# Two row blocks of a seven-product output step finished in their PSUM bank, and weight sums made four steps later

## The chip, the core and the metric

One core of a Trainium2 chip runs the whole program in one launch. The metric is device time in microseconds, the median of several runs; a profiled execution of the same program gives the traces. Engines are PE (matrix unit; PEld are its weight loads), DVE (vector), ACT (scalar), POOL (GpSimd) and SP (here only a queue that issues DMAs). Each works off its instructions in the order in which the program wrote them.

## What is computed

Attention with keys and values projected along the sequence, and behind it a gated feed-forward block:

```python
k_proj = einsum('ks,bhsd->bhkd', E, k)          # 1024 positions -> 64
v_proj = einsum('ks,bhsd->bhkd', F, v)
attn   = softmax(q @ k_proj^T / sqrt(64))       # 8 batches, 8 heads, 1024 x 64
x      = (attn @ v_proj), heads side by side    # 8192 rows x 512
g      = x @ w_gate                             # 512 -> 1536
out    = (g * sigmoid(g) * (x @ w_val)) @ w_out # 1536 -> 512, float32
```

## The kernel before

Rows are worked in 16 chunks c of 512 (`NC`), two to a batch. A chunk has 12 steps f (`NFT`), one for each 128 columns of the hidden layer, and the main loop counts them as t = 12c + f. In each step `f_g` makes four matmuls into the gate bank (`gps`, L462) and ACT the tanh `th` (L474); `f_v` makes four into the value bank (`vps`, L462), and DVE makes `s` (L481) from `th` and `gps` and `hT` (L486) from `s` and `vps`. There are two buffers for `gps` and two for `vps`, so the gate matmuls of step t need that `s` of step t-2 is done.

The order of everything else is written out by hand. `slots` holds, for two places in each step, the attention work of later batches: loads by POOL's DMA queue (`load_k`, `load_v`, `load_q`), key and value projections (`kvp`, L162), transposes by SP's DMA queue (`u_TD` makes `qTd`, `u_AD` makes `AT`), scores (`sc`, L353, `ee`), softmax sums on DVE (`zz` L368, `rr` L370), the scaling on POOL (`AAd`, L383) and the product with the values (`pv`, L410). `late` holds what runs after `f_v` of a step: the output product.

Chunk 0 takes its output product directly (`f_y`, L498, in t = 16 to 23). Chunks 1 to 15 take it as a 2 x 2 block product in seven block products instead of eight: the hidden layer in two halves and the output columns in two halves, the rows in two halves too. The sums of blocks that this needs are made ahead: of `w_out` by `w_sum` (`ws`, DVE, L526, five instructions for the whole run), of `hT` by `h_sum` (`hs`, L547; numbers 5 and 2 on POOL step by step, 1, 6 and 7 on DVE in the first steps of the next chunk). `f_m` takes one product per step while the next chunk is worked, n = 0 to 13: for each half p of the 128-row blocks the products 3, 4, 5, 2, 1, 6, 7, each six matmuls of 128x256 (`yps`, L564). With M1 to M7 for the products, the four output blocks are

```
C12 = M3 + M5          C21 = M4 + M2
C11 = M1 + M7 + M3 + M4 - C12      C22 = M1 + M6 + M3 + M4 - C21
```

In the kernel before, four banks' worth of products go through two PSUM banks, "y" and "z": X = [M3, M4] in y, Y = [M5, M2] in z, W = M1 in y, Z = [M7, M6] in z. `m_X` copies X to `xs` on ACT (L581) and adds its two halves to `tt` on POOL (L584); `m_Y` makes C12 and C21 on DVE (L590); `m_W` adds M1 to `tt` on DVE (L597); `m_Z` subtracts C12 and C21 from Z on DVE (`dd`, L603), and POOL adds `tt` to both (L604). SP then sends the four blocks (L610). Each of these stands right behind the product that completes its bank. The products stand in steps 0, 1, 2, 3, 4, 5, 5 for the first half and 6 to 11, 11 for the second, so that 6 and 7 share a step.

The last chunk has no chunk behind it: `f_m_last` makes its 14 products back to back, with the last additions of the first half on DVE, and of the second half in two pieces (L652, L658) whose rows ACT's DMA queue sends (L659).

The five `w_sum` stand in steps 2 to 6 of chunk 1. `wo` is `w_out` in SBUF, loaded by two DMAs on POOL's queue in the start-up.

Of the kernel before, what the change touches and what calls it, by code (L numbers as in the profile page):

```python
# [10 lines left out]
ALU = mybir.AluOpType  # L11
AX = mybir.AxisListType
BF16 = mybir.dt.bfloat16
FP32 = mybir.dt.float32
# [8 lines left out]
P = 128  # L23
# [5 lines left out]
CW = 512  # L29
# [3 lines left out]
HC = DM // 2  # L33
# [5 lines left out]
def kernel(  # L39
# [19 lines left out]
    nc = tc.nc  # L59
    scale = 1.0 / float(D) ** 0.5  # L60

    const = ctx.enter_context(tc.tile_pool(name="const", bufs=1))
# [6 lines left out]
    fw = ctx.enter_context(tc.tile_pool(name="fw", bufs=3))  # L69
    y_pool = ctx.enter_context(tc.tile_pool(name="ysb", bufs=2))  # L70
    d_pool = ctx.enter_context(tc.tile_pool(name="dsb", bufs=2))
# [4 lines left out]
    ps_a = ctx.enter_context(tc.tile_pool(name="psa", bufs=2, space=bass.MemoryType.PSUM))  # L76

    ident_bf = const.tile([P, P], BF16, name="ident_bf")
    ident_fp = const.tile([P, P], FP32, name="ident_fp")
    BD = [const.tile([P, H, P], BF16, name=f"BD{i}") for i in range(2)]  # L80
    BDV = [const.tile([P, NPAIR, P], BF16, name=f"BDV{i}") for i in range(2)]
    ks = [const.tile([P, H, D], BF16, name=f"ks{i}") for i in range(2)]
# [11 lines left out]
    def load_k(b, h0=0, h1=H):  # L94
        if b:
            kb[b] = kv_pool.tile([P, H, NJ, D], BF16, name="kb", tag="kb")
        nc.gpsimd.dma_start(
            out=kb[b][:, h0:h1].rearrange("p h j d -> p h (j d)"),
            in_=k[b, h0:h1].rearrange("h (p j) d -> p h (j d)", j=NJ),
        )  # L100
# [41 lines left out]
    def bank(where, shape, dt, name):  # L142
        if where == "a" and ring["wide"]:
            where = "aaz"[ring["n"] % 3]
            ring["n"] += 1
        pool, tag = banks[where]
        return pool.tile(shape, dt, name=name, tag=tag)
# [217 lines left out]
    def u_R(b, u):  # L365
        e = ee[b, u]
        z = aw.tile([P, 4, 2], FP32, name="zz", tag="zz", bufs=3)
        nc.vector.reduce_sum(out=z[:], in_=e[:], axis=AX.X)  # L368
        r = aw.tile([P, 4, 2], FP32, name="rr", tag="rr", bufs=4)
# [79 lines left out]
    half = {}  # L449
# [60 lines left out]
    def rows_of(c):  # L510
        b, ch = divmod(c, CH)
        return out[b * S : (b + 1) * S, :].rearrange("(p c j) d -> p c j d", c=CH, j=4)[:, ch]
# [38 lines left out]
            op=op,  # L551
        )

    def m_mm(c, p, m, ps):

        for f in range(HF):
            if m == 3:
                lhsT = hT[c][:, f, p * P : (p + 1) * P]
            elif m == 4:
                lhsT = hT[c][:, HF + f, HT + p * P : HT + (p + 1) * P]  # L560
            else:
                lhsT = hs[c, m][:, f, p * P : (p + 1) * P]
            rhs = {2: wo[:, f, 0:HC], 5: wo[:, HF + f, HC:DM]}.get(m)
            nc.tensor.matmul(  # L564
                out=ps,
                lhsT=lhsT,
                rhs=ws[m][:, f, :] if rhs is None else rhs,
                start=(f == 0),
                stop=(f == HF - 1),
            )  # L570

    ym = {}

    def m_bank(c, p, which, at):
        t = ym[c, p, which] = bank(at, [P, 2, HC], FP32, "yps")
        return t

    def m_X(c, p):

        xs = d_pool.tile([P, 2, HC], FP32, name="xs", tag="d")  # L580
        nc.scalar.copy(out=xs[:], in_=ym.pop((c, p, "X"))[:])  # L581
        ym[c, p, "xs"] = xs
        t = d_pool.tile([P, HC], FP32, name="tt", tag="t", bufs=2)
        nc.gpsimd.tensor_tensor(out=t[:], in0=xs[:, 0], in1=xs[:, 1], op=ALU.add)  # L584
        ym[c, p, "T"] = t

    def m_Y(c, p):

        ysb = ym[c, p, "y"] = y_pool.tile([P, 4, HC], FP32, name="ysb", tag="ysb")
        nc.vector.tensor_tensor(  # L590
            out=ysb[:, 1:3], in0=ym.pop((c, p, "xs"))[:], in1=ym.pop((c, p, "Y"))[:], op=ALU.add
        )

    def m_W(c, p):

        t = ym[c, p, "T"]
        nc.vector.tensor_tensor(out=t[:], in0=t[:], in1=ym.pop((c, p, "W"))[:, 0], op=ALU.add)  # L597

    def m_Z(c, p, eng=nc.gpsimd):

        d = d_pool.tile([P, 2, HC], FP32, name="dd", tag="d")
        ysb = ym[c, p, "y"]
        nc.vector.tensor_tensor(out=d[:], in0=ym.pop((c, p, "Z"))[:], in1=ysb[:, 1:3], op=ALU.subtract)  # L603
        eng.tensor_tensor(  # L604
            out=ysb[:, 0::3],
            in0=d[:],
            in1=ym.pop((c, p, "T"))[:].unsqueeze(1).to_broadcast([P, 2, HC]),
            op=ALU.add,
        )
        nc.sync.dma_start(  # L610
            out=rows_of(c)[:, p::2, :], in_=ym.pop((c, p, "y"))[:].rearrange("p (j x) d -> p j (x d)", j=2)
        )

    def f_m(c, n):

        p, n = divmod(n, 7)
        m = (3, 4, 5, 2, 1, 6, 7)[n]
        which, at, half = (
            ("X", "y", 0), ("X", "y", 1), ("Y", "z", 0), ("Y", "z", 1), ("W", "y", 0), ("Z", "z", 1), ("Z", "z", 0),
        )[n]  # L620
        if n in (0, 2, 4, 5):
            m_bank(c, p, which, at)
        m_mm(c, p, m, ym[c, p, which][:, half])
        if n in (1, 3, 4, 6):
            {1: m_X, 3: m_Y, 4: m_W, 6: m_Z}[n](c, p)

    def f_m_last(c):

        X = [m_bank(c, p, "X", "yg"[p]) for p in range(2)]
        Z = [m_bank(c, p, "Z", "a") for p in range(2)]  # L630
        Y = [m_bank(c, p, "Y", "vz"[p]) for p in range(2)]
        m_mm(c, 0, 3, X[0][:, 0])
        m_mm(c, 0, 6, Z[0][:, 1])
        m_mm(c, 1, 6, Z[1][:, 1])
        m_mm(c, 1, 3, X[1][:, 0])
        for p in range(2):
            m_mm(c, p, 4, X[p][:, 1])
            m_X(c, p)
        for p in range(2):
            m_mm(c, p, 5, Y[p][:, 0])  # L640
            m_mm(c, p, 2, Y[p][:, 1])
            m_Y(c, p)
        W = [m_bank(c, p, "W", "gv"[p]) for p in range(2)]
        m_mm(c, 0, 1, W[0][:, 0])
        m_W(c, 0)
        m_mm(c, 0, 7, Z[0][:, 0])
        m_mm(c, 1, 1, W[1][:, 0])
        m_Z(c, 0, nc.vector)
        m_W(c, 1)
        ysb, t = ym[c, 1, "y"], ym[c, 1, "T"]  # L650
        d = d_pool.tile([P, 2, HC], FP32, name="dd", tag="d")
        nc.vector.tensor_tensor(  # L652
            out=d[:], in0=t[:].unsqueeze(1).to_broadcast([P, 2, HC]), in1=ysb[:, 1:3], op=ALU.subtract
        )
        for x in (1, 0):
            if x == 0:
                m_mm(c, 1, 7, Z[1][:, 0])
            nc.vector.tensor_tensor(out=ysb[:, 3 * x], in0=d[:, x], in1=Z[1][:, x], op=ALU.add)  # L658
            nc.scalar.dma_start(  # L659
                out=rows_of(c)[:, 1 + 2 * x, :], in_=ysb[:, 2 * x : 2 * x + 2].rearrange("p x d -> p (x d)")  # L660
            )


    slots = defaultdict(list)
# [37 lines left out]
    with tc.manual_schedule():  # L702
# [3 lines left out]
        for i in range(2):  # L706
            nc.scalar.dma_start(
                out=kraw[i][:],
                in_=k[0, 2 * i : 2 * i + 2].rearrange("h (p j) d -> p h (j d)", j=NJ),
# [5 lines left out]
        nc.sync.dma_start(out=ef[0][:], in_=E)  # L715
        load_q(0, 0, (0, 2))
        load_k(0, 4, 8)
        zeros = const.tile([P, CW], BF16, name="zeros")
        nc.vector.memset(zeros[:], 0.0)
        make_identity(nc, ident_fp[:])  # L720
        make_identity(nc, ident_bf[:])
# [34 lines left out]
        for h in range(4):  # L756
            for n in range(2):
                eng = act if (h, n) == (3, 1) else dve
# [76 lines left out]
        for b in range(2, B):  # L835
            s0 = 48 * (b - 1) - (20 if b == 3 else 24)
            at = (43, 43, 44, 45) if b == 2 else (s0, s0 + 2, s0 + 4, s0 + 6)
# [9 lines left out]
        late = defaultdict(list)  # L847
        for n in range(NFT):
            late[NFT + 4 + (2 * n + 1) // 3].append((f_y, 0, n))
        for m, f in ((3, 2), (4, 3), (6, 4), (7, 5), (1, 6)):  # L850
            late[NFT + f].append((w_sum, m))
        for c in range(1, NC):
            for f in range(HF):
                for m in (5, 2):
                    late[c * NFT + HF + f].append((h_sum, c, m, f, f + 1))
            if c == NC - 1:
                late[c * NFT + HF].append((h_sum, c, 6, 0, HF, nc.vector))
                for f in (0, 2, 4):
                    for m in (1, 7):
                        late[c * NFT + HF + f + 1].append((h_sum, c, m, f, f + 2, nc.vector))  # L860
            else:
                for i, m in enumerate((1, 6, 7)):
                    late[(c + 1) * NFT + 1 + i].append((h_sum, c, m, 0, HF, nc.vector))
                for n, f in enumerate((0, 1, 2, 3, 4, 5, 5, 6, 7, 8, 9, 10, 11, 11)):
                    late[(c + 1) * NFT + f].append((f_m, c, n))

        for t in range(NIT):
            c, f = divmod(t, NFT)
# [5 lines left out]
            for fn, *a in late.pop(t, ()):  # L874
                fn(*a)
            run_slot(2 * t + 1)
        f_m_last(NC - 1)
        assert not slots and not late

# [28 lines left out]
```

## Time and profile before

| | |
|---|---|
| median of 3 runs | 556.84 us (556.82 to 557.48) |
| the profiled execution's own time | 556.68 us |
| its span, first to last instruction | 554.92 us |
| mean granted PE clock | 0.994 of full speed |
| busy: PE, DVE, ACT, POOL | 542.1, 428.5, 216.2, 291.6 us |
| PE instructions | 3500 matmuls, 3500 weight loads |
| HBM read, written | 60.29 MB, 16.78 MB |

A busy time is the sum of the durations of an engine's instructions without overlaps. A matmul's duration includes its way through the array (128x512 shows 0.378 us in the mean), while the next one starts after 0.216 us; so PE's pace is read from starts. In a timeline line the two numbers at the front are the start and the duration, and a bracket tells how long the engine was idle before and what ended that. A wait line gives the engine and line that waited, what released it, and then total, number and longest.

### The profile page before, as it was taken

The page shows a single profiled execution, that of the slowest core. Times are in us where ns is not written, and L with a number is a line of the kernel's source. Part 1 is how long each engine was busy: PE and PEld are TensorE (multiplying, and loading weights), DVE is VectorE, ACT ScalarE, POOL GpSimd, SP SyncE. Part 2 cuts the span into 40 slices and gives each one's busy share as a digit, 9 for nine tenths or more (in the row PEclk, how much of TensorE's full clock was granted, in tenths as well). Part 3 has the DMA queues.
Part 4 walks back from the last instruction along what each step waited for, and adds up shares of the span by engine and source line. Part 5 has one row for each costly group of instructions (what it writes and reads, how often), then busy time and mean ns, then how long its engine had stood idle before and what let it go on. Part 6 is the DMA issues. An engine that isn't in the chain of part 4 may idle for free.

```text
span 554.9 us, 9311 instructions
## 1 busy us (share of the span) xinstructions
PE 542.1 (98%) x3500; PEld 318.3 (57%) x3500; DVE 428.5 (77%) x726; ACT 216.2 (39%) x386; POOL 291.6 (53%) x364
## 2 busy tenths in 40 slices
PE   8999899999999999999999999999999999999995
PEld 4654355556556655556556655566655665555664
DVE  3785886779678875988669896788859887776894
ACT  3564343253435333453334424254244433333220
POOL 6851194376627835187443856258451763516162
PEclk9999899999999999999999999999999999999998
DMA  9999949918961599036970399313990212110012
GB/s 203 192 198 190 172 97 194 189 39 143 194 120 41 100 187 206 1 76 121 205 130 1 77 176 200 81 40 85 180 192 38 73 50 69 40 39 22 17 39 113
DMA packets 111613, 62.86 MB, mean 113 GB/s; under 512 B 65872, under 2 KB 102736, under 8 KB 111568
## 3 DMA queue, kind: packets, MB, share of 16 engines
q0 software_dynamic: 43952, 29.49, 37.2%
q1 hardware_dynamic: 66784, 31.20, 25.4%
q10 hardware_dynamic: 832, 1.57, 0.9%
q8 instruction: 27, 0.44, 0.3%
q14 instruction: 18, 0.15, 0.1%
HBM read 60.29 MB, written 16.78 MB: 139 GB/s over the span
## 4 chain that ended last, share of the span: by engine, by line
PE 87%; DMA 8%; POOL 2%; DVE 1%; issue 1%; ACT 0%; POOLq 0%; DVEq 0%
PE vps L462 27%; PE gps L462 27%; PE yps L564 24%; DMA wo<-in_moe_w_out_dram 4%; PE sc L353 2%; PE pv L410 2%; PE kvp L162 2%; PE yps L498 2%; DMA qb<-in_q_dram 2%; DMA Fraw<-in_F_dram 1%; DMA qTd<-qb 1%; POOL wv L126 1%; POOL wg L126 0%; POOL qb L116 0%; POOL AA L383 0%
## 5 line engine op out<-in xcount | busy, mean ns | idle before, releaser
L462 PE MATMUL vps<-xT,wv 128*128 128x512 bf16 (+1 forms) x776 | 198.2, 378 | 0.9 <-DMA wv<-in_moe_w_val_dram 0.9
L462 PE MATMUL gps<-xT,wg 128*128 128x512 bf16 (+1 forms) x772 | 196.5, 377 | 2.1 <-DVE s L481 2.1
L474 ACT ACTIVATE th<-gps 128x512 f32<-128x512 f32 x191 | 114.2, 598 | 203.9 <-PE gps L462 203.2
L481 DVE SCALAR_TENSOR_TENSOR s<-th,gps 128x512 f32<-128x512 f32 x191 | 128.6, 673 | 55.4 <-ACT th L474 53.9
L486 DVE SCALAR_TENSOR_TENSOR hT<-s,vps 128x512 bf16<-128x512 f32 x192 | 131.9, 687 | 21.0 <-DVE s L481 0.9
L547 POOL TENSOR_TENSOR hs<-hT 128x256 bf16<-128x256 bf16 x180 | 118.4, 679 | 39.7 <-DVE hT L486 38.9
L462 PEld LDWEIGHTS <-wv 128*128 128x128 bf16 x776 | 74.0, 98 | 84.5 <-issue 3.3
L564 PEld LDWEIGHTS <-hs 128*128 128x128 bf16 x900 | 88.0, 98 | 36.6 <-issue 2.5
L462 PEld LDWEIGHTS <-wg 128*128 128x128 bf16 x776 | 74.0, 98 | 58.2 <-issue 3.0
L383 POOL TENSOR_TENSOR AAd<-ee,rr 128x512 bf16<-128x512 f32 x56 | 58.5, 1046 | 73.9 <-ACT ee L357 36.4
L604 POOL TENSOR_TENSOR ysb<-dd,tt 128x512 f32<-128x512 f32 x28 | 35.7, 1274 | 88.4 <-DVE dd L603 88.4
L564 PE MATMUL yps<-ws,hs 128*128 128x256 bf16 x540 | 68.6, 273 | 2.4 <-DVE ysb L658 2.4
L150 ACT CAST xT<-pv 128x512 bf16<-128x512 f32 (+1 forms) x63 | 36.4, 581 | 48.4 <-PE pv L410 46.4
L584 POOL TENSOR_TENSOR tt<-xs 128x256 f32<-128x256 f32 x30 | 28.4, 947 | 39.4 <-ACT xs L581 39.2
L368 DVE TENSOR_REDUCE zz<-ee 128x8 f32<-128x512 f32 x64 | 43.3, 677 | 7.1 <-ACT ee L357 6.9
L564 PE MATMUL yps<-ws,hT 128*128 128x256 bf16 x360 | 48.8, 273 | 0.0
L564 PE MATMUL yps<-wo,hs 128*128 128x256 bf16 x360 | 48.6, 273 | 0.0
L547 DVE TENSOR_TENSOR hs<-hT 128x1536 bf16<-128x1536 bf16 (+1 forms) x49 | 46.3, 950 | 0.0
L357 ACT ACTIVATE ee<-sc 128x512 f32<-128x512 f32 x64 | 38.0, 598 | 16.5 <-PE sc L353 16.4
L564 PEld LDWEIGHTS <-hT 128*128 128x128 bf16 x360 | 35.2, 98 | 16.0
L581 ACT COPY xs<-yps 128x512 f32<-128x512 f32 x30 | 17.6, 586 | 31.9 <-PE yps L564 25.0
L590 DVE TENSOR_TENSOR ysb<-xs,yps 128x512 f32<-128x512 f32 x30 | 20.4, 680 | 3.5 <-ACT xs L581 2.8
(99 smaller groups left out, 318.9 us busy)
## 6 DMA issues: line engine op xcount, KB each, us to landing
out_dram<-ysb SPq DMA_DIRECT2D x29, 512.0 KB, 2.7
qb<-in_q_dram POOLq DMA_DIRECT2D x14, 512.0 KB, 18.2
kb<-in_k_dram POOLq DMA_DIRECT2D x7, 1024.0 KB, 9.7
vb<-in_v_dram POOLq DMA_DIRECT2D x7, 1024.0 KB, 14.9
wo<-in_moe_w_out_dram POOLq DMA_DIRECT2D x2, 768.0 KB, 21.4
kraw<-in_k_dram ACTq DMA_DIRECT2D x2, 512.0 KB, 4.8
qb<-in_q_dram POOLq DMA_DIRECT2D x4, 256.0 KB, 7.9
wg<-in_moe_w_gate_dram POOLq DMA_DIRECT2D x4, 256.0 KB, 7.7
```

Of the source, the lines that this page charges most:

```text
L150: (nc.scalar.copy if eng is nc.scalar else eng.tensor_copy)(out=out, in_=in_)
L357: nc.scalar.activation(out=e[:].rearrange("p h j k -> p (h j k)"), in_=ps[:].rearrange("p a k -> p (a k)"), func=AF.Exp, scale=scale,)
L368: nc.vector.reduce_sum(out=z[:], in_=e[:], axis=AX.X)
L383: eng.tensor_tensor(out=a.rearrange("p j h k -> p h j k"), in0=ee.pop((b, u))[:], in1=rr.pop((b, u))[:].unsqueeze(3).to_broadcast([P, 4, 2 ...
L462: nc.tensor.matmul(out=ps[:, ts], lhsT=(wg, wv)[w][:, kt, f * P : (f + 1) * P], rhs=x[:, kt, ts], start=(kt == 0), stop=(kt == NKT - 1),)
L474: nc.scalar.activation(out=th[:], in_=ps[:], func=AF.Tanh, scale=0.5)
L481: nc.vector.scalar_tensor_tensor(out=s1[:], in0=th[:], scalar=1.0, in1=g[:], op0=ALU.add, op1=ALU.mult)
L486: nc.vector.scalar_tensor_tensor(out=hT[c][:, f, :], in0=s1[:], scalar=0.5, in1=ps[:], op0=ALU.mult, op1=ALU.mult)
L547: eng.tensor_tensor(out=hs[c, m][:, fs, :], in0=quarter(hT[c], *a)[:, fs], in1=quarter(hT[c], *b)[:, fs], op=op,)
L564: nc.tensor.matmul(out=ps, lhsT=lhsT, rhs=ws[m][:, f, :] if rhs is None else rhs, start=(f == 0), stop=(f == HF - 1),)
L584: nc.gpsimd.tensor_tensor(out=t[:], in0=xs[:, 0], in1=xs[:, 1], op=ALU.add)
L604: eng.tensor_tensor(out=ysb[:, 0::3], in0=d[:], in1=ym.pop((c, p, "T"))[:].unsqueeze(1).to_broadcast([P, 2, HC]), op=ALU.add,)
```

## The change

Within a row half the products 5 and 2 are now added by PE onto 3 and 4 in the same bank, after ACT has copied the sums so far: the bank y then holds C12 and C21, and ACT copies them to the output tile (`m_52`). The bank z takes product 1, product 6 in its other half, and after `m_16` has read product 1, product 7 is added onto it. `m_16` makes `tt[1] = tt[0] + M1` on DVE and subtracts C12 and C21 from both halves of `tt` on POOL; `m_7` adds the bank z to that on DVE, and SP sends the rows. Product 6 moves one step ahead, to the step of product 1 (steps 4 and 10). In the last chunk both products 6 share a bank, and product 1 of each half has a bank of its own, onto which product 7 is added. The five `w_sum` move from steps 2 to 6 of chunk 1 to steps 6 to 10. `ident_fp` and `zeros`, which the start-up alone uses, move from tiles of their own into buffers of `th` and `s1`.

```diff
-    ident_fp = const.tile([P, P], FP32, name="ident_fp")
+    ident_fp = fw.tile([P, P], FP32, name="ident_fp", tag="th")
...
-    def m_mm(c, p, m, ps):
+    def m_mm(c, p, m, ps, start=False):
...
-                start=(f == 0),
+                start=(start and f == 0),
                 stop=(f == HF - 1),
+                skip_group_check=True,
...
-    def m_X(c, p):
-        xs = d_pool.tile([P, 2, HC], FP32, name="xs", tag="d")
-        nc.scalar.copy(out=xs[:], in_=ym.pop((c, p, "X"))[:])
-        ym[c, p, "xs"] = xs
-        t = d_pool.tile([P, HC], FP32, name="tt", tag="t", bufs=2)
-        nc.gpsimd.tensor_tensor(out=t[:], in0=xs[:, 0], in1=xs[:, 1], op=ALU.add)
-        ym[c, p, "T"] = t
-    def m_Y(c, p):
-        ysb = ym[c, p, "y"] = y_pool.tile([P, 4, HC], FP32, name="ysb", tag="ysb")
-        nc.vector.tensor_tensor(
-            out=ysb[:, 1:3], in0=ym.pop((c, p, "xs"))[:], in1=ym.pop((c, p, "Y"))[:], op=ALU.add
-        )
-    def m_W(c, p):
-        t = ym[c, p, "T"]
-        nc.vector.tensor_tensor(out=t[:], in0=t[:], in1=ym.pop((c, p, "W"))[:, 0], op=ALU.add)
-    def m_Z(c, p, eng=nc.gpsimd):
...
+    def m_34(c, p):
+        xs = d_pool.tile([P, 2, HC], FP32, name="xs", tag="d")
+        nc.scalar.copy(out=xs[:], in_=xx[c, p][:])
+        t = tt[c, p] = d_pool.tile([P, 2, HC], FP32, name="tt", tag="t")
+        nc.gpsimd.tensor_tensor(out=t[:, 0], in0=xs[:, 0], in1=xs[:, 1], op=ALU.add)
+    def m_52(c, p):
+        ysb = yo[c, p] = y_pool.tile([P, 4, HC], FP32, name="ysb", tag="ysb")
+        nc.scalar.copy(out=ysb[:, 1:3], in_=xx.pop((c, p))[:])
+    def m_16(c, p):
+        t = tt[c, p]
+        nc.vector.tensor_tensor(out=t[:, 1], in0=t[:, 0], in1=zz[c, p][:, 0], op=ALU.add)
+        nc.gpsimd.tensor_tensor(out=t[:], in0=t[:], in1=yo[c, p][:, 1:3], op=ALU.subtract)
+    def m_7(c, p):
+        ysb = yo.pop((c, p))
+        nc.vector.tensor_tensor(out=ysb[:, 0::3], in0=tt.pop((c, p))[:], in1=zz.pop((c, p))[:], op=ALU.add)
+        nc.sync.dma_start(
+            out=rows_of(c)[:, p::2, :], in_=ysb[:].rearrange("p (j x) d -> p j (x d)", j=2)
+        )
     def f_m(c, n):
         p, n = divmod(n, 7)
+        if n == 0:
+            xx[c, p] = m_bank("y")
+        if n == 4:
+            zz[c, p] = m_bank("z")
         m = (3, 4, 5, 2, 1, 6, 7)[n]
...
+        m_mm(c, p, m, (xx if n < 4 else zz)[c, p][:, int(m in (4, 2, 6))], m in (3, 1))
+        if n in (1, 3, 5, 6):
+            {1: m_34, 3: m_52, 5: m_16, 6: m_7}[n](c, p)
     def f_m_last(c):
...
+        xx[c, 0], xx[c, 1] = m_bank("y"), m_bank("g")
+        z6 = m_bank("a")
+        z1 = [m_bank("av"[p]) for p in range(2)]
+        for p in range(2):
+            m_mm(c, p, 3, xx[c, p][:, 0], start=True)
+        for p in range(2):
+            m_mm(c, p, 6, z6[:, p], start=(p == 0))
+        for p in range(2):
+            m_mm(c, p, 4, xx[c, p][:, 1])
+            m_34(c, p)
+        for p in range(2):
+            m_mm(c, p, 5, xx[c, p][:, 0])
+            m_mm(c, p, 2, xx[c, p][:, 1])
+            m_52(c, p)
+            d, ysb = tt[c, p], yo[c, p]
+            nc.vector.tensor_tensor(out=d[:, 1], in0=d[:, 0], in1=ysb[:, 2], op=ALU.subtract)
+            nc.vector.tensor_tensor(out=d[:, 0], in0=d[:, 0], in1=ysb[:, 1], op=ALU.subtract)
+            nc.vector.tensor_tensor(out=d[:, 1], in0=d[:, 1], in1=z6[:, p], op=ALU.add)
         for x in (1, 0):
+            for p in range(2):
+                m_mm(c, p, (7, 1)[x], z1[p][:, 0], start=(x == 1))
+                ysb = yo[c, p]
+                nc.vector.tensor_tensor(out=ysb[:, 3 * x], in0=tt[c, p][:, x], in1=z1[p][:, 0], op=ALU.add)
+                (nc.sync, nc.scalar)[p].dma_start(
+                    out=rows_of(c)[:, p + 2 * x, :], in_=ysb[:, 2 * x : 2 * x + 2].rearrange("p x d -> p (x d)")
+                )
...
-        zeros = const.tile([P, CW], BF16, name="zeros")
+        zeros = fw.tile([P, CW], BF16, name="zeros", tag="s1")
...
-        for m, f in ((3, 2), (4, 3), (6, 4), (7, 5), (1, 6)):
+        for m, f in ((3, 6), (4, 7), (6, 8), (7, 9), (1, 10)):
             late[NFT + f].append((w_sum, m))
...
-                for n, f in enumerate((0, 1, 2, 3, 4, 5, 5, 6, 7, 8, 9, 10, 11, 11)):
+                for n, f in enumerate((0, 1, 2, 3, 4, 4, 5, 6, 7, 8, 9, 10, 10, 11)):
                     late[(c + 1) * NFT + f].append((f_m, c, n))
```

## The prediction

> **What bounds the kernel now.** I read the page's engine rows and slices first, then the waits, the granted clock by windows, and the timeline at the places these point to. One PE step is called t, t = 12c + f; the seven products of a row half p are P3, P4, P5, P2, P1, P6, P7 (M3 and so on above), in that order.
>
> ```profile
> PE 542.1 (98%) x3500; PEld 318.3 (57%) x3500; DVE 428.5 (77%) x726; ACT 216.2 (39%) x386; POOL 291.6 (53%) x364
> ...
> PEclk9999899999999999999999999999999999999998
> ```
>
> PE is the bound: matmuls follow each other without a gap for nearly the whole span, so work taken off DVE, ACT or POOL is worth nothing unless PE waits for it. Two slices have a lower clock, the fifth and the last. The waits, all engines, show the only two PE stalls over 1.2 us and what DVE waits for:
>
> ```profile
> DVE ws L526 <- DMA wo<-in_moe_w_out_dram: 4.8, 1, 4.8
> ...
> PE yps L564 <- DVE ysb L658: 2.4, 1, 2.4
> PE gps L462 <- DVE s L481: 2.1, 1, 2.1
> ```
>
> The timeline at 55 us ties the first and the last of them together (columns: start, duration, engine, line, operation, tiles, count, idle before):
>
> ```profile
> 55.48 1.03 PE L498 MATMUL yps<-wo,hT 128*128 128x512 bf16 x4
> ...
> 57.04 0.96 DVE L526 TENSOR_TENSOR ws<-wo 128x1536 bf16<-128x1536 bf16 x1 [4.78 <-DMA wo<-in_moe_w_out_dram]
> 57.92 0.68 DVE L481 SCALAR_TENSOR_TENSOR s<-th,gps 128x512 f32<-128x512 f32 x1
> 58.65 1.02 PE L462 MATMUL gps<-xT,wg 128*128 128x512 bf16 x4 [2.14 <-DVE s L481]
> ```
>
> DVE is in order. The first weight sum waits for wo, s of t=15 stands behind it, the gate bank stays taken, and PE stops. Then the clock, by windows (the column after the five engines is the granted clock):
>
> ```profile
> 55.50:59.69 4.19, 2.05 (x10) 0.86 (x9) 2.54 (x4) 0.00 (x0) 0.00 (x0) 1.00 1.23 199
> 59.69:63.11 3.42, 3.42 (x9) 1.18 (x8) 3.23 (x7) 0.60 (x1) 0.00 (x0) 0.50 1.35 200
> 63.11:66.50 3.39, 3.39 (x23) 1.82 (x22) 3.29 (x6) 2.17 (x4) 0.00 (x0) 1.00 0.32 44
> ```
>
> Shortly after the stall PE runs at half its clock for 3.42 us, the only such stretch before the end of the work.
>
> **Weight sums four steps later.** Four matmuls of 128x512 take 0.863 us from start to start (58.65 to the next row's 59.51). Without the stall PE would go on at 55.48 + 0.86 = 56.34 instead of 58.65: 2.31 us. Half the clock for 3.42 us costs 1.71. Together 4.02 us; the same comes out of the work: from 55.48 to the first sc matmul at 63.79 lie 20 matmuls of 0.216, 4.32 us, and 8.31 passed. I take the whole of it, since the sums would now start near 63.4 us, 6 after wo has landed (the wait ends at 57.0).
> A rule speaks against counting the 1.71: the Trainium skill, "TensorE: Matmul & The Clock Gate", section "What's actually happening", has the clock halve only after at least one idle window of about 3.4 us. The stall is shorter than that, so by the page it would cost 2.31 alone and the sum below would be 555.1; the 0.50 row decides.
>
> What the sums now lie beside: DVE in t=18, 19, 21 and 22 has s 0.67, hT 0.69, two softmax rows of 0.68 + 0.20 and one sum of 0.95, 4.07 us, while PE's steps last 3.0, 3.7, 3.9 and 3.3 (gps starts 64.01, 67.05, 70.72, 74.64, 78.54, 81.85); t=20 has 3.1 against 3.9. DVE falls behind by 1.0, 1.4, 0.6, 0.8, 1.6 us. That is hidden: the bank that s(t) frees is wanted two steps later, about 4 us after s can run. Past that cover each us of lag would be one of PE.
>
> But PE arrives 4 us earlier at transfers. qTd of batch 1 is issued at 40.8 and lands 18.7 us later, at 59.5; PE now wants it at 59.8, just in time. vb of batch 2 is issued at 80.4, lands after 15.8, at 96.2, and the matmul that needs it starts at 96.2: no room. That DMA stands on POOL behind h_sum of t=21, which waits for hT(21). My hand timing of DVE (hT(18) 63.5, sum, two softmax rows, hT(19) 67.4, and so on) puts hT(21) at 74.5 where a shift of 4.0 would give 74.2. So the load moves 3.6 us and PE waits 0.4. Bounds: 0 and, if DVE were a whole us later, 1.4. **Net: -4.02 + 0.4.**
>
> **Products that go on in their bank.** Durations, groups with shapes kept apart:
>
> ```profile
> L590 DVE TENSOR_TENSOR ysb<-xs,yps 128x512 f32<-128x512 f32 x30 | 20.4, 680 | 3.5 <-ACT xs L581 2.8 <-PE yps L564 0.6
> L603 DVE TENSOR_TENSOR dd<-yps,ysb 128x512 f32<-128x512 f32 x29 | 19.9, 688 | 0.8 <-PE yps L564 0.2
> L581 ACT COPY xs<-yps 128x512 f32<-128x512 f32 x30 | 17.6, 586 | 31.9 <-PE yps L564 25.0 <-POOL hs L547 5.9 <-POOL AAd L383 1.0
> ...
> L597 DVE TENSOR_TENSOR tt<-tt,yps 128x256 f32<-128x256 f32 x30 | 12.4, 414 | 0.0
> ```
>
> Per row half, DVE loses the 0.68 of L590; L597 and L603 become m_16 and m_7, of the same sizes. ACT gains a copy of 0.586, 30 in all, 17.6 us; at 39% busy, and with 0.86 us of gate matmuls between P2 and the next tanh, it delays nothing. POOL keeps one operation of 128x512, which has no row: between 1.05 (L383, same elements) and 1.89 (twice the 0.947 of L584, whose elements are half); I take 1.27, the mean of L604, which has the same two f32 operands. PE has the same 3500 matmuls. Nothing of this is on the path; the new waits are.
>
> P5 now waits until ACT has copied P3 and P4. In before that copy ends 0.88 to 1.33 us ahead of the first matmul of P5 in all 28 row halves: nothing. P6 follows P1 at once, and P7 waits for m_16, which reads the bank that P7 adds to. Here it is tight; t=76 and 77:
>
> ```profile
> 230.68 0.82 PE L564 MATMUL yps<-ws,hs 128*128 128x256 bf16 x6
> ...
> 233.50 1.47 PE L564 MATMUL yps<-ws,hs 128*128 128x256 bf16 x12
> ...
> 234.49 0.41 DVE L597 TENSOR_TENSOR tt<-tt,yps 128x256 f32<-128x256 f32 x1
> ```
>
> The twelve are P6 and P7, six of 0.109 each: P7 starts at 233.50 + 0.65 = 234.15, and does so still when P6 has moved ahead, as the order between is only turned. L597 ends at 234.90, 0.75 too late. DVE has no gap over 0.12 us from 220.7 on, so without L590 (231.72 to 232.40, next start 0.60 later) it ends at 234.30; with 0.05 from DVE's end to PE's start (550.21 to 550.26 at the end) P7 waits 0.2. Of the 28, five are like this one (first halves of every second chunk); the rest have 0 to 1.2 us to spare even with L590 in place. **5 x 0.2 = +1.0**; bounds 0 and 5 x 0.8 = 4.0. Behind the waiting P7 stands all of PE, so this is paid in full. m_7 on DVE waits for POOL's subtraction, with s and hT of the next step behind it: L597 ends 2 us before L603 starts in most halves, 1.3 in the tightest, so 1.27 just fits; 1.89 would hold DVE 0.6 us in some halves, within the cover of 4 us.
> The rule that speaks against this part is in "PSUM — Partial Sum Buffer", section "PSUM bank collisions raise a hardware error": no two engines in one bank at once, so a reader and a product are to be parted by semaphores even on different halves. The trace agrees: at the end below, P7 waits 2.4 us for a reader of the other half.
>
> SP sends the rows after m_7, without the 1.27 of POOL that followed; its transposes queue behind that no later than now. ident_fp and zeros lie in buffers of th and s; their last readers run before the third th and s, so nothing waits.
>
> **The end.**
>
> ```profile
> 549.79 0.42 DVE L658 TENSOR_TENSOR ysb<-dd,yps 128x256 f32<-128x256 f32 x1
> ...
> 550.26 0.81 PE L564 MATMUL yps<-ws,hs 128*128 128x256 bf16 x6 [2.36 <-DVE ysb L658]
> ...
> 551.11 0.42 DVE L658 TENSOR_TENSOR ysb<-dd,yps 128x256 f32<-128x256 f32 x1 [0.91 <-PE yps L564]
> ```
>
> Now, by the same clock of 539.2 for the first of the 14 products: P5 of p=0 waits 0.24 for the copy that ends at 543.33, P2 of p=1 ends at 546.0, its copy at 546.8. DVE then does three operations of 0.42, with two gaps of 0.1: 548.3, and the two adds after P1, 548.7 and 549.2. P7 of p=0 waits for the first add: 548.8; both take 1.3, to 550.1, with 0.17 of pipeline 550.3, and the last add ends at 550.8 against 551.53. **-0.7**; bounds -0.95 without the gaps and 0 if the four transfers of 256 KB, issued within 2.1 us, crowd each other.
>
> **Sum:** profiled run 556.68 (span 554.92, 1.76 around it) - 4.02 + 0.4 + 1.0 - 0.7 = 553.4. The profiled run lies 0.16 under the median of 556.84, so I leave it there.
>
> **Rivals.** *Transfers take it back* (0.13): vb and qTd of batch 2 move little because DVE's lag holds POOL's issues. With half of the 4.0 returned at 96 us, 555.0; with all, 557.0. For: the landing at 96.2 with no room. Against: hT(21) loses only 0.3 by the count.
> *The half clock has another cause* (0.08): only 2.31 comes back, 555.1. Against: no other such stretch.
> *P7's wait is long* (0.12), the slower side: DVE at m_16 is later than before, held by m_7 behind POOL, and PE pays 28 times. The other terms give 4.3; it decides from 4.3 / 28 = 0.15 us per row half on. With DVE 0.8 later than in before, five halves wait 1.6 and eight others 0.3 to 0.8: about 12 us of wait, 564.5; half of that, 558.5. Against: DVE has 19 us less to do. That the weight sums would still meet wo needs a landing 6 us later; I give it nothing of its own.
>
> **How the numbers follow.** The forecast has 0.67, with a range of its own of 551.7 (no P7 wait, -0.95 at the end, no wait for vb) to 555.0. 0.2%, about what can be told from no change here, is 1.1 us. Faster: 0.67 + 0.08 + 0.05 of the first rival = 0.80; same 0.09; slower 0.11. The range goes up to 556.2, which leaves out the third rival and the worse part of the first.
>
> **What would show it.** Right: no wait of PE gps for s and no 0.50 stretch near 60 us; PE L564 waiting for L593 in about five places of 0.2; a wait for vb near 92 us; DVE about 409 busy, ACT 234. Wrong: P7 waits in most halves, or waits for DMA over 1 us that were not there.

## The result, and the profile after

The changed kernel takes 554.11 us (median; 553.93 to 554.18), the kernel before 556.85 beside it: a ratio of 0.9943, with a 95% interval of 0.9929 to 0.9957. It is 0.6% faster than the kernel before, and 0.7 us slower than the forecast of 553.4, inside the range. The profiled execution takes 554.06 (span 552.3) against 556.68 (554.92), so 2.62 us less.

The page first, engine rows and slices of the granted clock:

```profile
PE 537.3 (97%) x3438; PEld 317.9 (58%) x3500; DVE 414.1 (75%) x699; ACT 233.3 (42%) x416; POOL 294.5 (53%) x364
...
PEclk9999999999999999999999999999999999999999
```

(62 of PE's 3500 records are missing from this trace, so its 537.3 us are too few.) PE is still the bound, and neither the fifth slice nor the last has a lower clock. The waits of PE (engine and line that waited, releaser, total, number, longest):

```profile
PE yps L564 <- DVE ysb L640: 1.2, 1, 1.2
...
PE kvp L162 <- DMA vb<-in_v_dram: 0.9, 1, 0.9
```

The wait of `gps` for `s` (2.1) and DVE's 4.8 for `wo` are gone, the wait at the end is halved, and a wait for `vb` is new. Around 55 us the timeline of PE runs through, and the stretch that ran at half clock in the kernel before now has 1.00 (the column after the five engines):

```profile
55.38 1.03 PE L498 MATMUL yps<-wo,hT 128*128 128x512 bf16 x4
...
59.70 0.39 PE L353 MATMUL sc<-BD,qTd 128*128 128x128 bf16 x4
```

```profile
59.69:63.11 3.42, 3.37 (x25) 1.95 (x25) 1.89 (x4) 2.17 (x4) 0.95 (x1) 1.00 1.35 200
```

From `yps` at 55.38 to the first `sc` matmul at 59.70 now pass 4.32 us, exactly the twenty times 0.216 that the prediction counted; before it was 8.31.

Then the place where the forecast missed. At 92 us PE wants the keys and the values of batch 2; the bracket is idle time and its releaser:

```profile
92.06 0.40 PE L162 MATMUL kvp<-kb,ET 128*64 128x512 bf16 x1
...
93.33 0.38 PE L162 MATMUL kvp<-vb,FT 128*64 128x512 bf16 x1 [0.87 <-DMA vb<-in_v_dram]
...
103.65 0.40 PE L353 MATMUL sc<-BD,qTd 128*128 128x128 bf16 x4 [0.41 <-DMA qTd<-qb]
```

Both products use half of the array's columns, and in the kernel before their matmuls run side by side from 96.22 on, each pair 0.216 after the last. Here the second one starts 1.27 us after the first. `vb` has moved by 2.9 us only (landing at 93.29, against 96.18) where PE had moved by 4.2 (first `kb` matmul at 92.06, against 96.22).

The list of waits does not name the waits at P7. They are in the timeline, as a start that is too late; t = 77, all engines:

```profile
230.52 1.03 PE L462 MATMUL vps<-xT,wv 128*128 128x512 bf16 x4
...
231.13 0.41 DVE L593 TENSOR_TENSOR tt<-tt,yps 128x256 f32<-128x256 f32 x1
...
231.60 0.82 PE L564 MATMUL yps<-ws,hs 128*128 128x256 bf16 x6
```

Four matmuls from 230.52 on, 0.216 each, end the step's value product at 231.38; P7 starts at 231.60, 0.06 after L593 ends at 231.54. Most of the 0.21 between is hidden from the list because a matmul's duration includes its way through the array (1.03 for the four, to 231.55); only the 0.05 from there to 231.60 counts as idle.

The end, timeline of PE and DVE:

```profile
546.26 0.75 DVE L640 TENSOR_TENSOR ysb<-tt,yps 128x256 f32<-128x256 f32 x2
546.73 1.47 PE L564 MATMUL yps<-ws,hs 128*128 128x256 bf16 x12 [1.18 <-DVE ysb L640]
...
548.24 0.42 DVE L640 TENSOR_TENSOR ysb<-tt,yps 128x256 f32<-128x256 f32 x1 [0.23 <-PE yps L564]
```

The last addition starts at 548.24 against 551.11, 2.87 earlier; the last DMA takes 2.37 us from issue to landing (548.69 to 551.06) against 2.05 (551.57 to 553.62), which gives 0.3 back.

The starts of the gate weights' loads, step by step in the two traces, split the 2.62 us (after minus before; a row has everything since the row above it):

| where | forecast | measured | running difference |
|---|---|---|---|
| start-up | 0 | -0.10 | -0.10 |
| chunk 1, stall and half clock, to step 18 | -4.02 | -3.99 | -4.09 |
| products for `kb` and `vb` of batch 2, to step 30 | +0.4 | +1.17 | -2.92 |
| wait of `sc` for `qTd`, 0.49 before and 0.41 now, to step 32 | 0 | -0.08 | -3.00 |
| P7 in steps 53, 77, 101, 125, 149 (0.02 elsewhere) | 5 x 0.2 | 5 x 0.21 | -1.93 |
| the end | -0.7 | -0.69 | -2.62 |

(From step 29 on the difference also swings by 0.65 twice in each chunk, six matmuls of 0.109: that is P6 standing one step earlier, and it comes back in the next step.)

### The profile page after: what moved, and what is told of

The parts are those of the page before. It is cut to its first block, busy times and chain, and to the rows that moved or that the text cites. A ratio compares the mean times of both kernels' runs of the same rounds, so it can differ in the third digit from the quotient of the medians.

```text
span 552.3 us, 9270 instructions
## 1 busy us (share of the span) xinstructions
PE 537.3 (97%) x3438; PEld 317.9 (58%) x3500; DVE 414.1 (75%) x699; ACT 233.3 (42%) x416; POOL 294.5 (53%) x364
## 5 line engine op out<-in xcount | busy, mean ns | idle before, releaser
L462 PE MATMUL vps<-xT,wv 128*128 128x512 bf16 (+1 forms) x759 | 195.0, 377 | 2.5 <-DMA wv<-in_moe_w_val_dram 0.8
L462 PE MATMUL gps<-xT,wg 128*128 128x512 bf16 (+1 forms) x729 | 191.6, 377 | 1.9
L547 POOL TENSOR_TENSOR hs<-hT 128x256 bf16<-128x256 bf16 x180 | 120.6, 691 | 57.9 <-DVE hT L486 57.2
L594 POOL TENSOR_TENSOR tt<-tt,ysb 128x512 f32<-128x512 f32 x28 | 35.5, 1268 | 71.7 <-DVE tt L593 71.7
L357 ACT ACTIVATE ee<-sc 128x512 f32<-128x512 f32 x64 | 38.1, 598 | 18.5 <-PE sc L353 16.1
L588 ACT COPY ysb<-yps 128x512 f32<-128x512 f32 x30 | 17.6, 585 | 24.9 <-PE yps L564 21.6
```

The costliest lines, as they stand in the source:

```text
L357: nc.scalar.activation(out=e[:].rearrange("p h j k -> p (h j k)"), in_=ps[:].rearrange("p a k -> p (a k)"), func=AF.Exp, scale=scale,)
L462: nc.tensor.matmul(out=ps[:, ts], lhsT=(wg, wv)[w][:, kt, f * P : (f + 1) * P], rhs=x[:, kt, ts], start=(kt == 0), stop=(kt == NKT - 1),)
L547: eng.tensor_tensor(out=hs[c, m][:, fs, :], in0=quarter(hT[c], *a)[:, fs], in1=quarter(hT[c], *b)[:, fs], op=op,)
L594: nc.gpsimd.tensor_tensor(out=t[:], in0=t[:], in1=yo[c, p][:, 1:3], op=ALU.subtract)
```

## The experiments

Theory: moving the sums alone brings the 4 us, by taking idle time and half clock out of chunk 1; what is lost again is `vb`, late behind POOL, and five waits at P7; the products in their bank bring only the end. Rivals: the gain comes from a lighter DVE; the half clock has another cause; the wait for `vb` comes from POOL's new subtraction. The kernel before was timed in the same rounds as each of them, so ratios compare better than medians.

| kernel | median, us | before, us | ratio, 95% interval |
|---|---|---|---|
| the change | 554.11 | 556.85 | 0.9943 (0.9929 to 0.9957) |
| e1, sums alone | 553.83 | 557.01 | 0.9942 (0.9930 to 0.9955) |
| e2, products alone | 557.24 | 557.01 | 1.0005 (0.9996 to 1.0014) |
| e3, end of before | 554.92 | 557.01 | 0.9965 (0.9953 to 0.9978) |
| e4, P7 a step later | 553.21 | 557.01 | 0.9934 (0.9922 to 0.9947) |
| e5, stall filled | 557.33 | 556.87 | 1.0014 (1.0005 to 1.0022) |
| e6, sums spread | 552.90 | 556.87 | 0.9928 (0.9915 to 0.9941) |
| e8, one sum moved | 553.65 | 556.87 | 0.9945 (0.9933 to 0.9957) |
| e7, e4 and e6 | 551.87 | 556.87 | 0.9911 (0.9898 to 0.9923) |
| e9, e7 and DVE's order at the end | 551.47 | 557.26 | 0.9903 (0.9887 to 0.9919) |

**e1: only the weight sums are moved.** To the kernel before:

```diff
-        for m, f in ((3, 2), (4, 3), (6, 4), (7, 5), (1, 6)):
+        for m, f in ((3, 6), (4, 7), (6, 8), (7, 9), (1, 10)):
```

> The kernel before with only the five weight sums moved to steps 6 to 10. My account: the stall of 2.3 us and the half clock of 1.7 near 58 us go, and the wait for vb of batch 2 near 93 us comes with about 1.1 us, as in the changed kernel, because that comes from the sums alone: 554.0 us, no 0.50 stretch. Rival, that the gain of the changed kernel comes from DVE's lighter product work: 556.5 or more here. Rival, that the vb wait comes from POOL's new subtraction: 553.0, with hardly a wait for vb.

It gains as much as the whole change. The wait for `vb` is there too, in the waits of PE:

```profile
PE kvp L162 <- DMA vb<-in_v_dram: 0.6, 1, 0.6
```

There is no L594 in this kernel (and in the change the first one runs only behind 98 us), so the wait for `vb` comes with the moved sums and not with POOL's subtraction; and the 4 us need no lighter DVE. (By the starts, PE loses 0.95 there, against 1.24 in the change; what makes the other 0.3 was not followed.) The wait of 2.4 us before the last product stays.

**e2: only the products.** To the changed kernel:

```diff
-        for m, f in ((3, 6), (4, 7), (6, 8), (7, 9), (1, 10)):
+        for m, f in ((3, 2), (4, 3), (6, 4), (7, 5), (1, 6)):
```

> The changed kernel with the weight sums back at steps 2 to 6. My account: five waits of P7 of 0.21 us each (+1.05) and a shorter end (-0.7): 557.2 us against 556.85, with the stall and the 0.50 stretch near 58 us as before. Rival, that lighter DVE work is what gains: 555 or less. Rival, that the products cost nothing in the loop: 556.2.

No difference that can be measured: about 0.7 is won at the end and 1.05 lost at P7. The traced execution (556.66, the fastest of the eleven) also wins 0.44 in step 31, where the kernel before waits for `qTd`; that is why it is not slower than the kernel before's 556.68. Stall and half clock are back, in the waits and in the windows (the clock, 0.50, again after the five engines):

```profile
PE gps L462 <- DVE s L481: 2.4, 1, 2.4
```

```profile
59.18:62.60 3.42, 3.42 (x10) 1.21 (x8) 3.33 (x7) 0.60 (x1) 0.00 (x0) 0.50 1.31 202
```

**e3: the changed kernel with the last chunk's products of before.** `f_m_last`, cut to its core:

```diff
-            for p in range(2):
-                m_mm(c, p, (7, 1)[x], z1[p][:, 0], start=(x == 1))
...
+        o_W(c, 0)
+        m_mm(c, 0, 7, Z[0][:, 0], start=True)
+        m_mm(c, 1, 1, W[1][:, 0], start=True)
+        o_Z(c, 0, nc.vector)
+        o_W(c, 1)
...
+                m_mm(c, 1, 7, Z[1][:, 0], start=True)
```

> The changed kernel with the last chunk's end as in the kernel before. My account: the end is worth 0.7 us, so 554.8. The last product waits 2.4 us again for the reader of its bank. Rival, that the transfers at the end hide it: 554.1, no change.

The wait before the last product is back, and with it 0.8 us of the median:

```profile
PE yps L564 <- DVE ysb L689: 2.4, 1, 2.4
```

The intervals of e3 and of the change overlap a little (that of e3 begins at 0.9953, that of the change ends at 0.9957), so the size of the end's gain rests on the traces: 0.69 between the kernel before and the change, 0.68 between e3 and the change.

**e4: P7 of the first half one step later, beside P3 of the second.**

```diff
-                for n, f in enumerate((0, 1, 2, 3, 4, 4, 5, 6, 7, 8, 9, 10, 10, 11)):
+                for n, f in enumerate((0, 1, 2, 3, 4, 4, 6, 6, 7, 8, 9, 10, 10, 11)):
```

> The changed kernel with product 7 of each first row half one step later, in the step of the next half's product 3 (step 6). The reader that it waits for then has a whole step more. My account: the five waits of 0.21 go: 553.05 us, and no loss at steps 53, 77, 101, 125 and 149. Rival, that the 1.05 us between 106 and 538 us has another cause, such as the copies on ACT ahead of product 5: 554.1, and the losses stay where they are.

Timeline of PE at t = 78, where P7 now stands:

```profile
232.62 1.03 PE L462 MATMUL vps<-xT,wv 128*128 128x512 bf16 x3
233.48 0.82 PE L564 MATMUL yps<-ws,hs 128*128 128x256 bf16 x6
```

One of the four `vps` records is missing; 232.62 + 4 x 0.216 = 233.48, so P7 starts without a gap. Against the changed kernel the gate loads go from 0.14 later (step 52) to 0.90 earlier (step 190), 1.04 in all, in five equal parts at the five steps; five times 0.21 make 1.05. The ratios' intervals overlap; by the traces the five waits are real, and are avoided by giving `m_16` one step more.

**e5: the stall of before filled with work.** The sums stay where they were; in t = 17 ten matmuls on zeros stand before the gate matmuls. They are extra work, and nothing reads their result.

```diff
             i = 1 if t < 2 else None
+            if t == NFT + 5:
+                ps = bank("z", [P, CW], FP32, "warm")
+                for _ in range(10):
+                    nc.tensor.matmul(out=ps[:], lhsT=zeros[:, 0:P], rhs=zeros[:], start=True, stop=True)
             f_g(c, f, i)
```

> The kernel before with ten matmuls of 128x512 on zeros put into step 17 ahead of its gate matmuls, 2.16 us of PE work that the result does not use, in the place of the stall; the weight sums stay where they were. My account, that half the clock follows from PE's idle time: PE still reaches the gate matmul when s is done, the 0.50 stretch goes, and 1.7 us with it: 555.1 us. Rival, that the half clock has another cause: 556.85, with the 0.50 stretch in its place.

This was wrong: no gain, 557.33. The clock did what was expected; windows and timeline of e5:

```profile
58.60:62.00 3.40, 3.11 (x15) 1.46 (x15) 3.24 (x7) 0.60 (x1) 0.00 (x0) 1.00 1.28 203
```

```profile
56.04 2.32 PE L874 MATMUL warm<-zeros 128*128 128x512 bf16 x10
58.89 1.02 PE L462 MATMUL gps<-xT,wg 128*128 128x512 bf16 x4 [0.53 <-DVE s L481]
...
79.96 0.39 PE L410 MATMUL pv<-AT,BDV 128*128 128x512 bf16 x1 [1.26 <-DMA AT<-AAd]
```

The same product in the kernel before, which has no wait there to be seen:

```profile
79.68 0.39 PE L410 MATMUL pv<-AT,BDV 128*128 128x512 bf16 x1
```

The half clock is gone, and at step 18 PE stands 1.45 us ahead of the kernel before. It then loses 0.36 waiting for `s`, and 1.37 at step 22 waiting for `AT`. DVE had run just as late as before: its first sum starts at 57.28, when `wo` has landed (57.04 in the kernel before), and from there to 75 us it waits for nothing in both kernels, each instruction 0.24 later in e5; behind that stand POOL's `AAd` and SP's transpose, also 0.24 later (75.64 and 75.40). In both kernels the product with `AT` starts 22.6 to 22.7 us after that sum (57.04 to 79.68, 57.28 to 79.96). In the kernel before `AT` lands at 79.64, just as PE comes to it. So the 1.71 us at half clock had cost the kernel before nothing by itself: the chain through DVE ended at the same time. Only with the sums moved do PE and that chain come forward together; in the changed kernel `AT` is issued at 70.67, against 75.40.

**e6: the sums spread out,** in steps 5, 6, 10, 11, 12, so that none lies in t = 20 or 21:

```diff
-        for m, f in ((3, 6), (4, 7), (6, 8), (7, 9), (1, 10)):
+        for m, f in ((3, 5), (4, 6), (1, 10), (6, 11), (7, 12)):
```

> The changed kernel with the sums 3 and 4 one step earlier (steps 5 and 6) and the sums 1, 6 and 7 later (steps 10, 11 and 12), so that none stands on DVE between steps 18 and 21. My account: hT of step 21 is not late and POOL's h_sum of step 21 is not stretched, the loads of batch 2 are issued about 0.9 us earlier than in the changed kernel against PE, and the wait for vb shrinks from 1.1 to about 0.2: 553.2 us. Rival, that vb is held by the transfers and not by POOL: 554.1 and the same wait.

PE no longer waits for `vb`; its timeline has no bracket:

```profile
92.21 0.40 PE L162 MATMUL kvp<-vb,FT 128*64 128x512 bf16 x1
```

The load of `kb` is issued at 75.24, against 76.70 in the changed kernel, and that of `vb` right behind it.

**e8: one sum alone is taken out of t = 21.** This separates POOL's part of the delay from DVE's backlog:

```diff
-        for m, f in ((3, 6), (4, 7), (6, 8), (7, 9), (1, 10)):
+        for m, f in ((3, 6), (4, 7), (6, 8), (1, 10), (7, 11)):
```

> The changed kernel with the one weight sum 7 moved from step 9 to step 11. hT of step 21 is as late as in the changed kernel, but no weight sum runs on DVE beside POOL's h_sum of that step. My account: its first half takes 0.67 us and not 1.32, the loads go out 0.65 earlier, and the wait for vb falls by as much: 553.45 us. Rival, that the lateness of hT alone makes the wait: 554.1, and h_sum takes 1.3 again.

POOL and DVE in the changed kernel at t = 21, and then POOL in e8:

```profile
74.65 0.95 DVE L526 TENSOR_TENSOR ws<-wo 128x1536 bf16<-128x1536 bf16 x1
...
74.82 1.95 POOL L547 TENSOR_TENSOR hs<-hT 128x256 bf16<-128x256 bf16 x2 [0.17 <-DVE hT L486]
76.70 0.94 POOL L97 DMA_DIRECT2D kb<-in_k_dram  x1
```

```profile
74.64 1.30 POOL L547 TENSOR_TENSOR hs<-hT 128x256 bf16<-128x256 bf16 x2 [0.17 <-DVE hT L486]
75.88 0.94 POOL L97 DMA_DIRECT2D kb<-in_k_dram  x1
```

```profile
PE kvp L162 <- DMA vb<-in_v_dram: 0.3, 1, 0.3
```

Without a sum of DVE beside them the two additions on POOL take 1.30 and not 1.95, the load of `kb` is issued 0.82 earlier (0.18 of that is the earlier start), and PE waits 0.3 where the change waits 0.9. The time does not separate e8 from the change (0.9945 and 0.9943, though 0.5 us lie between the medians); the traces do, and e6, in the same rounds as e8, is 0.75 us faster.

**e7: e4 and e6 together.**

> The changed kernel with product 7 of the first halves one step later and the sums spread as in the run before: the two gains do not touch each other, so 554.1 - 1.0 - 0.9 = 552.2 us. Rival, that they overlap: 553.

551.87: the changed kernel less 1.05 for P7 and 1.17 for `vb` would be 551.89. The two losses are apart and add up.

**e9: e7 with another order of DVE's instructions in the last chunk.** P1 and P7 of both halves are made in pairs; DVE adds M1 before it has subtracted C12, which lets P7 go earlier, and subtracts C12 only while PE makes P7 (`sub`, `six` and `add` are the three kinds of operation that were there):

```diff
+        for p in range(2):
+            m_mm(c, p, 1, z1[p][:, 0], start=True)
+        sub(0, 1), six(0), sub(1, 1), add(0, 1), six(1), add(1, 1)
+        for p in range(2):
+            m_mm(c, p, 7, z1[p][:, 0])
+        sub(0, 0), sub(1, 0), add(0, 0), add(1, 0)
```

> The best so far (product 7 of the first halves one step later, sums spread; 551.87 us) with the last chunk's additions on DVE in another order: the two subtractions that only the very last additions need come after the first additions, so that product 7 waits for fewer of them. My account: PE's wait of 1.18 us at the end falls to 0.4 or less and the last addition comes 0.6 to 0.8 us earlier: 551.2 us. Rival, that the four transfers at the end set the time and not the additions: 551.9, with the wait gone.

Timeline of the end, e7 and then e9:

```profile
544.49 1.47 PE L564 MATMUL yps<-ws,hs 128*128 128x256 bf16 x12 [1.18 <-DVE ysb L640]
```

```profile
543.35 1.66 PE L564 MATMUL yps<-ws,hs 128*128 128x256 bf16 x12 [0.22 <-DVE ysb L642]
...
544.73 0.74 DVE L642 TENSOR_TENSOR ysb<-tt,yps 128x256 f32<-128x256 f32 x2
```

PE's wait falls from 1.18 to 0.22, and the last DMA is issued 0.95 earlier (545.50 against 546.45). Of that 0.19 stood already at the last gate load, so the new order is worth 0.76, as expected. The DMA lands 0.63 earlier (548.15 against 548.78): the last two transfers are closer together, and the last takes 2.65 us where it took 2.33. The rival of this experiment, that transfers take it back, was right for 0.3 us. At 551.47 this is the fastest version, a ratio of 0.9903 (0.9887 to 0.9919); its gain over e7, 0.4 in the medians, is shown by the traces and not by the intervals.

## Why the prediction was right, and where it was not

**Weight sums, -4.02: right in size (-3.99), right in the place, wrong in its reading, so right in part by luck.** The chain from `wo` over DVE to PE was as described, e1 shows that it is the whole gain, and the half clock does come from the idle time (e5). But the prediction took 2.31 and 1.71 for two sums that each stand for themselves. e5 shows that they do not: half the clock fell into time in which PE would have waited for `AT` instead. The sum of 4.0 held because the edit released both chains. The rule weighed there put the halving after a whole idle window, 3.4 us: the kernel before and e2 show it after 2.14 and 2.40 us of idle PE, and e5 shows it gone when that time is filled; its alternative, 555.1 by not counting the 1.71, was not what happened.

**The wait for `vb`, +0.4: right mechanism, the term that was mis-sized.** It came to 1.17 (1.24 lost in step 28, less 0.07 that the kernel before had lost in step 22). The failing step is "the load moves 3.6 us". hT(21) ended at 74.74, 0.24 later than the hand timing, and POOL's two additions, taken at the durations of before, took 0.65 more beside DVE's sum. 3.6 - 0.24 - 0.65 = 2.7, and `kb` was issued 2.78 earlier (76.70), against this row of the kernel before:

```profile
79.48 0.94 POOL L97 DMA_DIRECT2D kb<-in_k_dram  x1
```

The prediction listed what the sums lie beside on DVE, and not what they lie beside on POOL; e8 and e6 show that this was the difference. The 0.77 more than explain the 0.7 by which the forecast was too low.

**P7, +1.0: right.** Five places, the five predicted, 0.21 each; the other 23 row halves show nothing. That the list of waits would show them was wrong: all but 0.05 of each lies under the modelled tail of the matmul ahead.

**Copies and subtraction at nothing: right.** ACT came to 233.3 us (234 forecast), POOL's subtraction to its assumed size of 1.27 us:

```profile
L594 POOL TENSOR_TENSOR tt<-tt,ysb 128x512 f32<-128x512 f32 x28 | 35.5, 1268 | 71.7 <-DVE tt L593 71.7
```

DVE's busy time fell by 14.4 us and not by 19. The durations by themselves fell by 18.5, although the weight sums took 1.19 us in the mean instead of 0.95 (1.2 in all); but busy time leaves out overlaps, and with 27 instructions fewer behind each other there is 4.1 less overlap to leave out (22.9 before, 18.8 now).

**The end, -0.7: right (-0.69),** but in part by luck: the last addition came 0.94 earlier, which was the bound without gaps, the transfers took 0.3 of that back, which was the other bound's reason, and 0.07 came behind the last landing.

**The rivals.** That transfers take the gain back was the nearest: by 0.77 us more than forecast, not by half of it. That the half clock has another cause than PE's idle time is excluded by e5. A long wait at P7 did not come.

## What to carry to other kernels

When an instruction is moved in an engine that works in order, look at what it will lie beside on *every* engine, and at the DMA issues that are queued behind those. Do not price a stretch of slow clock or a stall from PE's row alone: fill it, or ask which other chain ends just behind it, because PE may only arrive earlier at the next wait. Waits that are about as short as the tail of a matmul hardly show in a list of waits; compare the starts of a repeated instruction, step by step.

## What the runs showed of the hardware

- **An addition on POOL stands still while DVE sums two tensors in SBUF.** `hs` on POOL (128x256, bf16) takes 0.65 to 0.67 us alone and 1.32 to 1.39 where DVE's sum of 128x1536 (0.95 us) began just before it; with a weight sum this happened once in the kernel before (two in 1.95 us from 68.88, beside a sum at 68.72), in the changed kernel at 63.4, 67.6, 71.7 and 74.8. It also goes the other way: the last weight sum of the changed kernel begins at 78.63, 0.10 behind POOL's `AAd` (1.06 us from 78.53), and takes 1.84. The Trainium skill, "SBUF — State Buffer", section "SBUF: two separate sides", describes it: the port pair that these two engines share is locked by whichever starts first, for its whole instruction, and the other stands still. The trace agrees to 0.13 us: DVE's sum ends at 75.60, two additions of 0.65 after that would end at 76.90, and they end at 76.77.
- **2.14 us of idle PE were enough for half the clock, and then for 3.42 us of it.** The kernel before (2.14 idle by the bracket; PE starts 2.31 late) and e2 (2.40) show 0.50 for one stretch of 3.42; with the gap filled down to 0.53 (e5) the clock stays at 1.00, as it does after the 1.18 at the end of the changed kernel. In every trace here the clock changes only at whole multiples of 3.413 us after it first rose (16 of them in the kernel before, at 59.69 us). Cut into such stretches, none with up to 1.98 us of idle PE is followed by 0.50 (the changed kernel, 546.77 to 550.18), and one with 2.14 is (the kernel before, 56.28 to 59.69); that the idle share of such a stretch decides is read from these cases and was not tested by itself. The Trainium skill, "TensorE: Matmul & The Clock Gate", section "What's actually happening", has an idle window of about 3.4 us before the clock halves; the length of the slow stretch agrees with that figure, the idle time needed was less.
- **The last transfer of 256 KB takes longer the closer it follows the one before it:** from issue to landing 2.05 us when it is issued 1.33 behind that one (the kernel before), 2.33 and 2.37 at 0.66 behind (e7 and the changed kernel), 2.65 at 0.34 (e9).
